# The two-level stage of a transformer block on one core: operands loaded six units ahead, level-1 differences a unit earlier, chunk loads a unit earlier, normalisation tiles overlapped

## The chip, the cores and the metric

The kernel runs on one core of one Trainium2 chip. The metric is the device time of one execution in microseconds (us), the median of several runs. A profiled execution of the same program gives the trace that is read here. The engines are TensorE (PE: matmuls; PEld: its weight loads), VectorE (DVE), ScalarE (ACT), GpSimd (POOL) and SyncE (SP), whose queue issues all DMAs.

## The reference

One block: layer norm with a modulation, an attention with a memory over four segments, a residual; a second layer norm, a gated feed-forward (GEGLU), a residual. Everything is float32. The change lies in the second half.

```python
def _B_ref(x, w_gate, w_up, w_down):        # x 2048 x 1024, F = 3584
    return (_gelu(x @ w_gate) * (x @ w_up)) @ w_down

mod = (_silu(c) @ w_mod).reshape(c.shape[0], 6, 1, -1)
sa, ca, ga, sb, cb, gb = (mod[:, 0], mod[:, 1], mod[:, 2], mod[:, 3], mod[:, 4], mod[:, 5])
h = _layernorm(x, axis=-1) * (1 + ca) + sa
x = x + ga * _A_ref(h, A_wq, A_wk, A_wv, A_wo, A_beta)
h = _layernorm(x, axis=-1) * (1 + cb) + sb
x = x + gb * _B_ref(h, B_w_gate, B_w_up, B_w_down)
```

## The kernel before

**Precision.** Every matmul operand is split into an upper half (a ScalarE copy to fp32r) and a lower half (source minus upper half, on VectorE or GpSimd); three matmuls make one product. `cut` and `put_two` do this; `put_two` issues the lower half only behind the next operand's upper half (`owed`, `settle`).

**Fast multiplication.** gate and up are computed with a scheme of seven products instead of eight (Strassen's in Winograd's form), numbered 1 to 7 and worked in the order `ROUND` = 1, 5, 6, 2, 7, 3, 4. Four of the seven products of the outer level are carried out with a second level inside; that is the stage here, `two(n)` for n = 0 to 27, called a **unit**. Units 0 to 13 work on the operand pair 1 and 2 (the first pair), units 14 to 27 on the pair 5 and 6 (the second). A unit is 14 products of 6 matmuls, 84 in all: for each r in `ROUND` one product for each operand of the pair. It ends in four partial results per operand, which go to DRAM (`st_d`). In a second-pair unit the sums continue from base values loaded back from there (`base_load`, tiles `y`). Behind the stage come 56 **chunks** (`gate_up(u)`), 36 matmuls each, for the outer level's products 7, 3 and 4, and then `down()`.

**What sets the order.** The program is written out by Python generators. `sides` is a list of them; `step()` runs behind every product and advances each by one `yield`. So a `yield` is a step of 6 matmuls, and 14 steps are a unit. `later(k, f)` calls f k steps on. PE's, VectorE's, ScalarE's, GpSimd's and SP's instructions stand in the order in which they are written, and each engine works its queue in that order. An instruction that waits holds all that stand behind it on its engine, and this holds for DMAs on SP.

The parts that the change touches:
- `norm_steps`, with `wait=6`: the second layer norm of the last segment, four token tiles, beside units 1 to 5. One tile is loaded, scaled, transposed on PE in two halves (`turn`, tiles `tpc` in the single PSUM bank `o`) and evacuated to `htc` by ScalarE (first half) or VectorE (second half).
- `mixes`: sums and differences of the normalised rows for both levels, stored to DRAM as `mix_d`: `a_mix(0)`, `a_mix(1)` (when the norm is done), `a_mix_two` (those of the second pair).
- `a_second`: loads the second pair's 14 operands of 512 KB (tiles `w`) and splits each into two, 28 in all (`AA`). An operand takes the place of a first-pair operand when unit 13 has used it (`done`).
- `b_two(n)` makes unit n's weights (`BB`) beside unit n - 1 from raw rows `g` and calls `seven`, whose four sums GpSimd makes. For the second pair GpSimd first takes the level-1 differences of up and gate (with `gh`) and stores one of them (`t2_d`).
- `a_last`: the chunks' operands (`ra`, split to `A`); `gu_load`: a chunk pair's raw weights (`ru`, `rg`); `b_part`: their splits (`B`); `cg_load`: a chunk's three partial results (`cg`).

## Time and profile before

| what | us |
|---|---|
| median of 3 runs (2709.99 to 2714.82) | 2712.97 |
| the profiled execution, its own time | 2714.43 |
| its span | 2712.5 |
| start of unit 1, 13, 14, 15 | 1142.29, 1386.91, 1410.61, 1451.94 |
| start of chunk 0, of `down()` about | 1702.52, 2191.7 |

The page gives the busy time of each engine over the span, the chain of waits (followed back from the last instruction to what released each), and groups of like instructions by line. `out<-in` are tile names without numbers; x12 is a count. In a row of waits stand the total, the number of times and the longest; in a timeline the start, the duration and, in brackets, the idle time before and what ended it; in a table of windows the busy time (count) of each engine, then the granted TensorE clock, the DMA engines' share and GB/s. The time of the whole is set by TensorE where it has matmuls ready; where it waits, the last releaser is what counts.

### The profile page before, as it was taken

To read this page: it belongs to the slowest core of one execution; us is meant where nothing else is said; L and a number is where in the kernel's file an instruction comes from. 1 tells how busy PE (TensorE), PEld (TensorE's weight loads), DVE (VectorE), ACT (ScalarE), POOL (GpSimd) and SP (SyncE) were. 2 spreads that over 40 slices of the span, in tenths; PEclk is the share of its full clock that TensorE was granted. 3 is DMA by queue.
4 is the path that set the end of the run, shared out by engine and by line. 5 is a ranking of instruction groups with operands and counts; after the bars stand their busy time and mean duration, and the time that the engine had idled before them with its cause. 6 is when DMAs were issued, how large, how long until landed. Compare 5 with 4: busy or idle time off the path is not lost.

```text
span 2712.5 us, 42405 instructions
## 1 busy us (share of the span) xinstructions
PE 2644.9 (98%) x13905; PEld 2193.3 (81%) x13905; DVE 1746.8 (64%) x3681; ACT 1377.4 (51%) x3163; POOL 1046.6 (39%) x1586
## 2 busy tenths in 40 slices
PE   7999999999999999999998999899999999999999
PEld 6788888888888788777876888688888888888887
DVE  6676656766677745767775555677777554575456
ACT  6778767776767634555553334433333333233323
POOL 4233334433343532334456665387787300000000
PEclk9999999999999999999998999899999999999999
DMA  7355444435443567577887777899999896786563
GB/s 264 103 157 159 116 135 141 144 102 159 114 133 99 174 213 245 185 258 259 284 313 255 271 273 273 324 358 370 361 360 366 297 342 222 270 296 202 184 209 123
DMA packets 284187, 617.81 MB, mean 228 GB/s; under 512 B 28992, under 2 KB 53568, under 8 KB 283968
## 3 DMA queue, kind: packets, MB, share of 16 engines
q1 hardware_dynamic: 283968, 615.13, 67.4%
q8 instruction: 109, 1.79, 0.3%
q14 instruction: 110, 0.90, 0.1%
HBM read 378.56 MB, written 186.12 MB: 208 GB/s over the span
## 4 chain that ended last, share of the span: by engine, by line
PE 47%; DMA 3%; DVE 2%; issue 1%; ACT 1%; POOL 0%; SPq 0%; ACTq 0%; DVEq 0%; POOLq 0%
PE y L1647 19%; PE f L1446 16%; PE pb L1226 5%; PE pa L1226 3%; PE pc L1226 3%; DMA w<-mix_d 1%; DMA cg<-st_d 0%; DMA wr<-gd_d 0%; DMA rg<-wg 0%; DVE y L1254 0%; ACT BB L934 0%; DMA ra<-mix_d 0%; DMA rm<-h_d 0%; DMA ru<-wu 0%; DMA hid_d<-g 0%
## 5 line engine op out<-in xcount | busy, mean ns | idle before, releaser
L1647 PE MATMUL y<-B,L 128*128 128x512 f32 x2352 | 533.9, 389 | 0.5 <-DVE L L931 0.5
L1647 PEld LDWEIGHTS y<-B,L 128*128 128x128 f32 x2352 | 441.3, 188 | 93.0 <-DVE L L931 1.2
L1446 PE MATMUL f<-A,B 128*128 128x512 f32 x2016 | 462.7, 391 | 9.2 <-DVE A L931 7.0
L1446 PEld LDWEIGHTS f<-A,B 128*128 128x128 f32 x2016 | 380.0, 189 | 91.7 <-DVE A L931 9.8
L619 ACT ACTIVATE sj<-sj,mm 128x384 f32<-128x384 f32 (+3 forms) x512 | 281.0, 552 | 41.0 <-DVE mm L617 40.5
L706 POOL TENSOR_SCALAR_AFFINE_SELECT pt<-pt 128x128 f32<-128x128 f32 x512 | 166.8, 347 | 331.5 <-ACT pt L705 323.5
L617 DVE CUSTOM_DVE_ANT_0 sj<-S,mask 128x384 f32<-128x384 f32 (+3 forms) x512 | 228.2, 488 | 98.5 <-PE S L615 71.5
L1226 PE MATMUL pb<-AA,BB 128*128 128x512 f32 x1008 | 252.6, 397 | 16.6 <-POOL AA L931 4.5
L705 ACT ACTIVATE pt<-T 128x256 f32<-128x256 f32 (+3 forms) x512 | 182.3, 444 | 133.1 <-PE T L703 126.5
L1226 PEld LDWEIGHTS pb<-AA,BB 128*128 128x128 f32 x1008 | 190.1, 190 | 64.4 <-DVE AA L931 5.1
L934 ACT ACTIVATE L<-X 128x512 fp32r<-128x512 f32 x168 | 105.8, 630 | 259.1 <-PE y L1647 170.4
L931 DVE TENSOR_TENSOR L<-X,L 128x512 fp32r<-128x512 f32 x168 | 115.9, 691 | 147.1 <-ACT L L934 147.1
L394 POOL TENSOR_TENSOR w<-r,w 128x256 fp32r<-128x256 f32 x180 | 133.7, 773 | 141.4 <-ACT w L388 139.0
L1473 ACT ACTIVATE g<-f 128x512 f32<-128x512 f32 x56 | 33.5, 598 | 287.6 <-PE f L1446 287.6
L403 PE MATMUL kv<-w,hha 128*128 128x256 f32 x896 | 173.8, 284 | 2.2 <-DVE vx L421 2.2
L1226 PE MATMUL pc<-AA,BB 128*128 128x512 f32 x672 | 164.8, 393 | 2.3 <-DVE AA L931 2.2
L1226 PE MATMUL pa<-AA,BB 128*128 128x512 f32 x672 | 164.0, 392 | 0.9 <-DVE AA L931 0.9
L931 DVE TENSOR_TENSOR BB<-g,BB 128x512 fp32r<-128x512 f32 x112 | 91.2, 815 | 95.8 <-ACT BB L934 95.5
L1226 PEld LDWEIGHTS pc<-AA,BB 128*128 128x128 f32 x672 | 126.5, 189 | 30.2 <-DVE AA L931 3.3
L1226 PEld LDWEIGHTS pa<-AA,BB 128*128 128x128 f32 x672 | 126.7, 189 | 28.6 <-DVE AA L931 1.7
L931 POOL TENSOR_TENSOR t_a<-g,t_a 128x256 f32<-128x256 f32 x112 | 91.0, 832 | 150.9 <-DVE BB L931 129.2
L403 PEld LDWEIGHTS kv<-w,hha 128*128 128x128 f32 x896 | 143.9, 191 | 3.4 <-DVE vx L421 2.5
(295 smaller groups left out, 5442.6 us busy)
## 6 DMA issues: line engine op xcount, KB each, us to landing
B<-wc_d SPq DMA_DIRECT2D x112, 512.0 KB, 4.1
cg<-st_d SPq DMA_DIRECT2D x168, 256.0 KB, 6.4
st_d<-x SPq DMA_DIRECT2D x112, 256.0 KB, 2.7
st_d<-y SPq DMA_DIRECT2D x112, 256.0 KB, 2.3
hid_d<-g SPq DMA_DIRECT2D x56, 512.0 KB, 5.9
wc_d<-T SPq DMA_DIRECT2D x56, 512.0 KB, 5.0
X<-hid_d SPq DMA_DIRECT2D x112, 256.0 KB, 4.6
wr<-gd_d SPq DMA_DIRECT2D x84, 256.0 KB, 4.2
```

Of the source, the lines that this page charges most:

```text
L394: nc.gpsimd.tensor_sub(w[:, 1, c], r[:, c], f32(w[:, 0, c]))
L403: nc.tensor.matmul(ps, b[:, sl], w[:, a], start=(kt == 0 and a == 0 and b is hi), stop=(kt == KT - 1 and a == 1), **kw)
L617: nc.vector.tensor_tensor_reduce(out=sj[:, :nv], in0=ps[:, :nv], in1=mask[:, L - nv:], scale=-1.0, scalar=3.4e38, op0=ALU.add, op1=ALU.min ...
L619: nc.scalar.activation(sj[:, :nv], sj[:, :nv], AF.Exp, bias=mm[:, j, i:i + 1], scale=-1.0, accum_out=ll[:, i, j:j + 1])
L705: nc.scalar.activation(pt, ps[:, nn - n:nn], AF.Exp)
L706: nc.gpsimd.affine_select(pt[:, :P], pt[:, :P], pattern=[[1, P]], compare_op=ALU.is_ge, fill=0.0, base=0, channel_multiplier=-1)
L931: f(*xs)
L934: nc.scalar.activation(hi, src, AF.Copy)
L1226: nc.tensor.matmul(ps, w[:, a, at:at + P], A["a", i, r, k][b], start=(r in (1, 5) and k == a == b == 0), stop=(k == 1 and a == 1), skip_gr ...
L1446: nc.tensor.matmul(ps, B[fc, i][:, a, kt * P:(kt + 1) * P], A[p, i, kt][b], start=False, stop=(kt == 3 and a == 1), skip_group_check=True)
L1473: nc.scalar.activation(h2_, pb, AF.Gelu_apprx_tanh)
L1647: nc.tensor.matmul(banks[t], ops[k][:, y, t * P:(t + 1) * P], B[slots[k]][:, x], start=(i not in (2, 4, 3) and j == 0 and x == 0 and y == ...
```

## The change

- **Normalisation:** the next tile's load moves behind this tile's scaling, the halves' transposes stand four steps apart instead of two, and a tile takes 12 steps instead of 17.
- **Second-pair operands:** `a_second` starts five steps behind the end of `mixes` instead of at unit 13, keeps six operands loaded instead of four (two of each six in pairs of `c` tiles), and makes all lower halves on VectorE.
- **Level-1 differences:** a generator of their own, `b_one`, run beside unit n for unit n + 2; in `seven` the third sum of the second pair goes to a temporary instead of over a raw row.
- **GELU and its store** of the first pair's gate: one step later.
- **Ends:** the first four `ra` loads are issued ahead of unit 26, the second chunk pair's raw weights ahead of unit 27, and the middle partial result of the first two chunks with the other two, in a temporary; weights of a unit are finished (`flush`) at its end in all units.

The numbers of lines in the diff and in the rows below are those of each version.

```diff
@@ norm_steps
         if wait:
             for q in range(len(toks)):
-                while stored.get(toks[q]) != 2:
-                    yield
-                load(q)
-                for _ in range(wait):
-                    yield
+                if q == 0:
+                    load(q)
+                    for _ in range(wait):
+                        yield
...
                 norm_scale([t], mv, rs, nm)
-                for _ in range(wait - 2):
+                if q + 1 < len(toks):
+                    load(q + 1)
+                for _ in range(4):
                     yield
-                for h in range(2):
-                    turn(q, h)
+                turn(q, 0)
+                for _ in range(4):
                     yield
-                    yield
+                turn(q, 1)
+                yield
             return
@@ mixes
             yield from a_mix_two()
+            mixed.append(1)
+
+        mixed = []
+
+        def second():
+
+            while not mixed:
+                yield
+            for _ in range(5):
+                yield
+            ff["first"] = a_second()
+            yield from ff["first"]
@@ a_second
-                    t = (ra_tile if q % 4 > 1 else lambda n: pair_tile(n, "U"))(f"w{i}_{r}")
...
+                    if q % 6 > 3:
+                        rs.append([c_tile(f"w{i}_{r}_{c}") for c in range(2)])
+                        for c in range(2):
+                            nc.sync.dma_start(rs[-1][c], src[c * P:(c + 1) * P])
+                        return
+                    t = ra_tile(f"w{i}_{r}") if q % 6 > 1 else flat(pair_tile(f"w{i}_{r}", "U"))
...
-            for _ in range(4):
+            for _ in range(6):
                 load()
...
-                    put_two(i, r, c, rs[q][:, c], nc.gpsimd if c and i == 5 and r in (2, 7, 3, 4) else nc.vector)
+                    put_two(i, r, c, rs[q][c], nc.vector)
@@ b_two, b_one, seven
-            if n >= NJ:
-                for q in (1, 0):
-                    u, g, k = raw[q], raw[2 + q], (2 * (n % NJ) + q) * P
-                    diff(u[:, :L], u[:, :L], g)
-                    yield
-                    diff(u[:, L:], u[:, L:], u[:, :L])
-                    later(1, lambda u=u, k=k: nc.sync.dma_start(t2_d[k:k + P], u[:, L:]))
-                    yield
-                if n + 1 < 2 * NJ:
-                    later(2, lambda: b_two_load(n + 1))
...
-            yield from seven(b11, b12, b21, b22, t1, t2_, put)
+            yield from seven(b11, b12, b21, b22, t1, t2_, put, t1 if n >= NJ else b12)
+
+        def b_one(n):
+
+            b_two_load(n)
+            for _ in range(5):
+                yield
+            for q in range(2):
+                u, g, k = two_raws[n][q], two_raws[n][2 + q], (2 * (n % NJ) + q) * P
+                diff(u[:, :L], u[:, :L], g)
+                yield
+                diff(u[:, L:], u[:, L:], u[:, :L])
+                later(1, lambda u=u, k=k: nc.sync.dma_start(t2_d[k:k + P], u[:, L:]))
+                yield
...
-            diff(b12, b22, b12)
+            diff(t3, b22, b12)
@@ two
-                later(2, lambda: nc.scalar.activation(t, t, AF.Gelu_apprx_tanh))
-                later(3, put)
+                later(3, lambda: nc.scalar.activation(t, t, AF.Gelu_apprx_tanh))
+                later(4, put)
...
-                    cg_load(int(r == 3), (0, 2))
+                    cg_load(int(r == 3), (0, 2, 1))
@@ cg_load
-                t = c_tile(f"cg{q}_{u}") if at < 2 and q != 1 else a_tile(
+                t = tmp_tile(f"cg{q}_{u}") if u < 2 and q == 1 else c_tile(f"cg{q}_{u}") if at < 2 and q != 1 else a_tile(
@@ the loops over units and chunks
                 sides.append([mixes(), 1, "m"])
+                sides.append([second(), 1])
+            if NJ - 2 <= n < 2 * NJ - 2:
+                sides.append([chain(wait_for(3 if n >= NJ else 0), b_one(n + 2)), 1, "o"])
...
             if n == NJ - 1:
                 flush("m")
-                ff["first"] = a_second()
-                sides.append([ff["first"], 1])
...
+            if n == 2 * NJ - 2:
+                following.append(a_last())
+                next(following[0])
             if n == 2 * NJ - 1:
-                following.append(a_last())
                 sides.append([following[0], 1])
-            if 0 < n < NJ - 1:
+            if 0 < n < NJ - 2:
                 b_two_load(n + 2)
-            elif n == 2 * NJ - 2:
-                gu_load(0)
+            elif n >= 2 * NJ - 2:
+                gu_load(n - 2 * NJ + 2)
             two(n)
-            if n < NJ - 1:
-                flush("b")
+            flush("b")
+            flush("o")
         for u in range(NU):
             fc, p = divmod(u, 2)
             if p == 0 and fc + 1 < FC:
+                sides.append([b_part(fc + 1), 1, "b"])
                 if fc + 2 < FC:
                     gu_load(fc + 2)
-                sides.append([b_part(fc + 1), 1, "b"])
-            if u == 0:
-                cg_load(0, (1,))
-                cg_load(1, (1,))
```

**SP's queue around the second pair's first loads** (`w`, the name's first number is r; `st_d` stores of unit 12's results, `t_d` the stored level-1 differences). Before:

```order
L1000 DMA mix_d_76<-u_1_0_17047 128x512
L1263 DMA st_d_73<-y_1_17108 128x512
L1263 DMA st_d_74<-x_0_17142 128x512
L1121 DMA w_1_17236<-mix_d_70 128x2x512
L1121 DMA w_1_17238<-mix_d_70 128x2x512
L1121 DMA w_5_17240<-mix_d_75 128x2x512
L1121 DMA w_5_17242<-mix_d_76 128x2x512
L1263 DMA st_d_74<-y_0_17154 128x512
L1162 DMA t_d<-g_1_17052 128x512
L1121 DMA w_6_17290<-mix_d_75 128x2x512
```

and now:

```order
L1014 DMA mix_d_76<-u_1_0_16953 128x512
L1285 DMA st_d_73<-x_0_17150 128x512
L1196 DMA t_d<-g_0_17070 128x512
L1140 DMA w_1_17167<-mix_d_70 128x2x512
L1140 DMA w_1_17169<-mix_d_70 128x2x512
L1140 DMA w_5_17171<-mix_d_75 128x2x512
L1140 DMA w_5_17173<-mix_d_76 128x2x512
L1136 DMA w_6_0_17175<-mix_d_75 128x512
L1136 DMA w_6_1_17176<-mix_d_75 128x512
L1285 DMA st_d_74<-x_1_17105 128x512
L1196 DMA t_d<-g_1_17071 128x512
```

The loads stand ahead of seven of unit 12's eight result stores instead of behind seven, six operands deep (two more of unit 13's operand 6 follow the last `w` row shown), but behind the store of a level-1 difference, `t_d<-g_0`.

**GpSimd's queue in unit 14** (`g` level-1 differences, `t_a` sums in `seven`, `AA` lower halves of operands; x2 is the two halves of a row). Before:

```order
L931 TENSOR_TENSOR g_1_17338<-g_1_17338,gh_1_17343 128x256 x2
L931 TENSOR_TENSOR AA_2_1_1_17477<-w_2_17367,AA_2_1_0_17476 128x256 x2
L931 TENSOR_TENSOR g_1_17338<-g_1_17338 128x256 x2
L931 TENSOR_TENSOR g_0_17337<-g_0_17337,gh_0_17340 128x256 x2
L931 TENSOR_TENSOR g_0_17337<-g_0_17337 128x256 x2
L931 TENSOR_TENSOR t_a_17551<-g_1_17338,g_0_17337 128x256 x2
L931 TENSOR_TENSOR AA_7_1_1_17548<-w_7_17431,AA_7_1_0_17547 128x256 x2
L931 TENSOR_TENSOR t_a_17552<-g_1_17338,t_a_17551 128x256 x2
L931 TENSOR_TENSOR g_1_17338<-g_1_17338 128x256 x2
L931 TENSOR_TENSOR AA_3_1_1_17625<-w_3_17497,AA_3_1_0_17624 128x256 x2
L931 TENSOR_TENSOR t_a_17552<-g_0_17337,t_a_17552 128x256 x2
L931 TENSOR_TENSOR AA_4_1_1_17674<-w_4_17573,AA_4_1_0_17673 128x256 x2
```

and now:

```order
L933 TENSOR_TENSOR t_a_17510<-g_1_17263,g_0_17262 128x256 x2
L933 TENSOR_TENSOR t_a_17511<-g_1_17263,t_a_17510 128x256 x2
L933 TENSOR_TENSOR t_a_17510<-g_1_17263 128x256 x2
L933 TENSOR_TENSOR t_a_17511<-g_0_17262,t_a_17511 128x256 x2
L933 TENSOR_TENSOR g_0_17567<-g_0_17567,gh_0_17570 128x256 x2
L933 TENSOR_TENSOR g_0_17567<-g_0_17567 128x256 x2
L933 TENSOR_TENSOR g_1_17568<-g_1_17568,gh_1_17573 128x256 x2
L933 TENSOR_TENSOR g_1_17568<-g_1_17568 128x256 x2
```

The four `AA` rows are gone to VectorE; the differences that unit 14's GpSimd makes are no longer those that its own sums `t_a` need but those of the unit behind.

**SP's queue between unit 27 and chunk 1** (`ru`, `rg` raw weights; `cg` partial results; `ra` operands). Before, from the middle of the first group of raw weights:

```order
L1347 DMA rg_19960<-wg 128x512
L1348 DMA rg_19960<-t_d 128x512
L1340 DMA cg_1_19964<-st_d_73 128x512
L1340 DMA cg_1_19966<-st_d_74 128x512
L1340 DMA cg_0_19968<-st_d_73 128x512
L1340 DMA cg_1_19970<-st_d_73 128x512
L1340 DMA cg_2_19972<-st_d_73 128x512
L1263 DMA st_d_74<-y_0_19786 128x512
L1346 DMA ru_19988<-wu 128x1024
L1347 DMA rg_19989<-wg 128x512
L1348 DMA rg_19989<-t_d 128x512
L1316 DMA ra_4_0_20004<-h_d 128x2x512
```

and now:

```order
L1338 DMA ra_3_1_19966<-mix_d_71 128x2x512
L1368 DMA ru_19972<-wu 128x1024
L1369 DMA rg_19973<-wg 128x512
L1370 DMA rg_19973<-t_d 128x512
L1362 DMA cg_0_19977<-st_d_73 128x512
L1362 DMA cg_1_19979<-st_d_73 128x512
L1362 DMA cg_2_19981<-st_d_73 128x512
L1285 DMA st_d_74<-y_0_19798 128x512
L1338 DMA ra_4_0_20010<-h_d 128x2x512
L1338 DMA ra_4_1_20039<-h_d 128x2x512
```

One group of raw weights and two `cg` loads have left this place; they stand in unit 27.

8 lines of the change are left out of this document (4 added, 4 removed).

## The prediction

> **What bounds the kernel now.** I read the page first, for the engine that is always busy.
>
> ```profile
> span 2712.5 us, 42405 instructions
> PE 2644.9 (98%) x13905; PEld 2193.3 (81%) x13905; DVE 1746.8 (64%) x3681; ACT 1377.4 (51%) x3163; POOL 1046.6 (39%) x1586
> ```
>
> TensorE (PE) is busy for 98%, so only time that PE loses can be won. The change touches the stage of 28 units (line 1226) and the first two chunks behind it. I cut that stretch with the table of windows at the starts of units 1, 13, 14 and 15, of the chunk stage, and of its first undisturbed run of matmuls.
>
> ```profile
> core 0: us, PE busy (x) PEld busy (x) DVE busy (x) ACT busy (x) POOL busy (x), PEclk, DMA share, GB/s
> 1142.29:1386.91 244.62, 235.61 (x1042) 191.27 (x1040) 169.29 (x252) 134.36 (x249) 113.30 (x127) 1.00 0.80 275
> 1386.91:1410.61 23.70, 20.09 (x86) 15.45 (x84) 14.42 (x21) 12.76 (x25) 10.27 (x12) 1.00 0.90 306
> 1410.61:1451.94 41.33, 28.17 (x85) 18.38 (x84) 30.23 (x37) 20.23 (x38) 33.40 (x37) 0.78 0.79 276
> 1451.94:1702.52 250.58, 250.58 (x1097) 206.35 (x1096) 143.80 (x205) 99.25 (x180) 148.66 (x184) 1.00 0.77 271
> 1702.52:1732.94 30.42, 21.27 (x72) 14.63 (x70) 18.01 (x26) 12.80 (x24) 7.37 (x8) 0.78 0.89 337
> ```
>
> The chain of waits gives the price of a group of 12 matmuls:
>
> ```profile
> 1282.74 2.72 PE pb L1226 x12
> 1285.46 2.72 PE pc L1226 x12
> ```
>
> A unit is 84 matmuls, so 7 x 2.72 = 19.04 us; one step (6 matmuls) is 1.36 us. Against that:
> - **Start**, units 1 to 12: 244.62 - 12 x 19.04 = 16.1 us too long. Eight groups of transposes at about 0.41 us (1162.85 to 1163.26 below) are 3.3 of it; 12.8 us are lost.
> - **Pair change**, units 13 and 14: 23.70 + 41.33 = 65.03 us instead of 38.08; 26.95 us lost. The granted clock of 0.78 in unit 14 is inside this sum.
> - Units 15 to 27: no loss (PE busy all 250.58 us).
> - **End**: 70 matmuls (70 x 0.2267 = 15.87 us) take 30.42 us; 14.55 us lost.
>
> Together 54.3 us are to be had. PE's waits name the releasers:
>
> ```profile
> PE tpc L269 <- ACT htc L278: 7.1, 4, 2.6
> PE f L1446 <- DVE A L931: 7.0, 4, 3.9
> PE pb L1226 <- POOL AA L931: 4.5, 1, 4.5
> PE pb L1226 <- DVE AA L931: 3.4, 3, 1.7
> PE pb L1226 <- ACT x L1250: 2.5, 1, 2.5
> PE f L1446 <- ACT A L934: 2.1, 1, 2.1
> ```
>
> **Part 1, the normalisation (start).** PE's timeline shows one token tile:
>
> ```profile
> 1162.85 0.66 PE L269 MATMUL tpc<-ident,nc 128*128 128x128 f32 x4 [0.47 <-ACT nc L248]
> 1163.26 3.01 PE L1226 MATMUL pa<-AA,BB 128*128 128x512 f32 x12
> 1168.51 0.66 PE L269 MATMUL tpc<-ident,nc 128*128 128x128 f32 x4 [2.24 <-ACT htc L278]
> ```
>
> The second half's transposes need the single "o" bank, which ScalarE empties of the first half 1168.51 - 1163.26 = 5.25 us after its transposes. Before, 12 matmuls (2.72 us) stand between the halves, and PE waits for the rest. Now 24 stand there (5.44 us), so the waits of 7.1 us go but for about 0.2 us. ScalarE's GELU also moves one step back, so that it is less often blocked there. The tile takes 12 steps instead of 17; its work is the same and lies under matmuls. **Term: -7** (bounds -3, if the denser work makes the evacuations later, to -9, if some of the unnamed 5 us go too). The mixed operands are stored 11 steps sooner (60 steps of the first mix instead of 71 of the normalisation stand before the second mix); the next part needs that.
>
> **Part 2, the pair change.** Here is what the 28 second-pair operands (AA, 14 loads of 512 KB) cost now; ScalarE's and POOL's timelines, the queue's, and four pieces of the chain:
>
> ```profile
> 1391.46 2.01 SPq L1121 DMA_DIRECT2D w<-mix_d  x4
> 1397.25 0.63 ACT L1015 ACTIVATE AA<-w 128x512 fp32r<-128x512 f32 x1 [3.85 <-DMA w<-mix_d]
> 1419.54 1.87 POOL L931 TENSOR_TENSOR AA<-w,AA 128x256 fp32r<-128x256 f32 x2 [5.44 <-ACT AA L1015]
> ...
> 1391.46 5.76 DMA w<-mix_d
> 1406.53 7.75 DMA w<-mix_d
> 1423.28 4.05 DMA t_d<-g
> 1434.81 7.94 DMA w<-mix_d
> ```
>
> The loads are issued 4.5 us into unit 13, four deep, and ScalarE, which is in order, stands behind them; later loads wait for one of four buffers, land 7.75 and 7.94 us after issue, and four lower halves queue on POOL behind level-1 differences that wait for DMAs. The change answers each: the first loads are emitted at about step 8 of unit 12 instead of the first step of unit 13, six steps (8 us) sooner, so that the first should land near 1397.25 - 8 = 1389.2, 2.3 us into unit 13; a load is issued five operands (10 steps, 13.6 us) before its use instead of three (8.2 us), against landings of at most 7.94 us; the lower halves all go to VectorE; the differences come a unit earlier, in a temporary that the store does not hold. The extra four DMAs cost an issue each (w x4 above: 2.01 / 4 = 0.5 us) on SP, which has room.
>
> What is late next is **VectorE**. In the new order 56 VectorE instructions stand from the first lower half to the last. They may run from about 2.5 us into unit 13 (first landing) until one step before the end of unit 14: 38.08 - 2.5 - 1.4 = 34.2 us. Their mean is not known beforehand; the nearest rows are 14.42 / 21 = 0.687 us (POOL busy 43%) and 30.23 / 37 = 0.817 us (POOL busy 81%). That is 38.5 to 45.8 us, 4.3 to 11.6 too many; POOL's 16 instructions a unit will lie between, so I take the middle, 8, and 1 us for one hand-over from ScalarE to VectorE (0.63 and 0.69 us) at the last operands. Of the 26.95 us, 9 stay. **Term: -18** (bounds -23, with 4.3 us left, to -13, with 14 left should loads be late too). The DMA engines set a similar floor:
>
> ```profile
> DMA packets 9428, 18.66 MB, mean 287 GB/s; under 512 B 848, under 2 KB 848, under 8 KB 9424
> 1800.00:1850.00 50.00, 50.00 (x222) 41.42 (x221) 33.04 (x40) 18.63 (x36) 37.09 (x40) 1.00 0.99 372
> ```
>
> Units 13 and 14 moved 18.66 MB. Less six early loads (3.1 MB), 15.5 MB at 372 GB/s (the rate of a full window) take 41.7 us: 3.6 over, below VectorE's 47.
>
> **Part 3, the end.**
>
> ```profile
> 1709.39 4.21 SPq L1340 DMA_DIRECT2D cg<-st_d  x5
> 1717.29 1.00 SPq L1316 DMA_DIRECT2D ra<-h_d  x2
> 1716.63 0.69 DVE L1470 TENSOR_TENSOR g<-cg,cg 128x512 f32<-128x512 f32 x1 [5.42 <-DMA cg<-st_d]
> 1717.98 3.78 PE L1446 MATMUL f<-A,B 128*128 128x512 f32 x8 [3.93 <-DVE A L931]
> 1715.25 5.81 DMA ru<-wu
> 1722.66 0.63 ACT L934 ACTIVATE B<-ru 128x512 fp32r<-128x512 f32 x1 [8.79 <-POOL ru L931]
> 1726.86 4.22 PE L1446 MATMUL f<-A,B 128*128 128x512 f32 x9 [2.21 <-DVE A L931]
> ```
>
> Two late loads hold everything: part 1 of the first chunk (VectorE waits 5.42 us with A's lower halves behind it) and the raw weights of the next chunk (ScalarE waits 8.79 us with A's upper halves behind it). Both are now issued in unit 27, before 1702.52 and so at least 7 us sooner; both in-order queues run on. Late next is the last operand, ra_4 of the second half: it was issued at 1717.29; five fewer DMAs stand ahead of it, at 4.21 / 5 = 0.84 us each 4.2 us, so I expect 1713.1 and, with 4.1 us (the base load's landing in the steady units, quoted under C) to land and 1.3 us to split, 1718.5, when its product could start at 1702.52 + 5 x 2.72 = 1716.1. About 2.5 us stay. **Term: -12** (bounds -8, with two waits of 3 us left, to -14). The four ra loads move into unit 26; 2.1 MB more on 271 GB/s x 19 us = 5.1 MB stays under 372 x 19 = 7.1 MB.
>
> **Edits at nothing.** In units 15 to 26 POOL keeps 16 instructions a unit (148.66 us of 250.58) and now waits for VectorE before it overwrites a temporary; VectorE idles 43% there and PE waits for neither. If that cover failed, rival C is its price. The early flush only empties generators that are done by then.
>
> Sum: 7 + 18 + 12 = 37 us off the profiled execution's 2714.43 us; that is 1.5 us above the median of the runs (2712.97), so **2676 us**. The terms' bounds give 24 to 46 us, 2667 to 2689.
>
> **Rivals.** A, *VectorE against POOL*. The nearest row for an instruction with both operands in SBUF while POOL works is 1205 ns:
>
> ```profile
> L1254 DVE TENSOR_TENSOR y<-y,x 128x512 f32<-128x512 f32 x3 | 3.6, 1205 | 0.1
> L931 DVE TENSOR_TENSOR AA<-w,AA 128x512 fp32r<-128x512 f32 x24 | 21.0, 883 | 6.0 <-ACT AA L1015 6.0
> ```
>
> If all 43 such instructions of the 56 (28 AA, 13 BB, 2 sums) took that, 43 x 1.205 + 13 x 0.683 = 60.7 us, 26.5 over: part 2 gives nothing, 2694 us. Against it: AA's mean was 883 ns with POOL at 81%. 8%. The Trainium skill's page "SBUF — State Buffer", section "SBUF: two separate sides", says that VectorE with two SBUF inputs and GpSimd share a port as an exclusive lock, the loser waiting for the whole instruction; by that rule the halves moved off POOL would pay up to A's price. The trace agrees that the wait exists (1205 against about 683 ns) and not that each pays it.
>
> B, *the loads do not come sooner*. In the new order they stand behind a store of a level-1 difference, which waits for POOL. If that holds SP as long as the before's start of 1391.46, only POOL's own 4.5 us and some of the rest go, part 2 gives 8 us: 2686 us. For it: SP is in order. Against: POOL was busy only 10.27 of 23.70 us in unit 13, and that difference is its sixth of about eight in unit 12. 10%.
>
> C, *slower*: the difference's store, at step 10 of a unit, holds SP in units 15 to 26 until the base sums' load (step 2 of the next unit, used five steps = 6.8 us later) is late. That needs a hold of over six steps, 8.2 us; then each of 12 units would wait for one landing of a base load,
>
> ```profile
> y<-st_d SPq DMA_DIRECT2D x44, 256.0 KB, 4.1
> SPq L1162 <- POOL t_a L931: 2.1, 7, 0.3
> ```
>
> 12 x 4.1 = 49 us, more than the 37 gained: 2725 us. Against: from 1460 to 1680 those stores held SP 2.1 us in all. 4%.
>
> **How the numbers follow.** Forecast 76%, A 8%, B 10%, C 4%, 2% for what I do not see. The range 2666 to 2695 takes in the bounds, A and B. What a measurement can tell from no change is about 0.2% (5.4 us). Faster 0.94 (forecast, A, B), same 0.02, slower 0.04 (C).
>
> **What would show it.** Part 1 is right if PE's wait for htc falls from 7.1 to under 1 us. Part 2: units 13 and 14 take about 47 us together, ScalarE no longer waits for w near the start of unit 13, POOL no longer appears as PE's releaser, and VectorE is busy almost throughout. Part 3: the wait of 5.42 us for cg and of 8.79 us for ru are gone, and the 70 matmuls take 18 to 19 us. Units 15 to 27 must still be 250 us. It is wrong if the two units still take over 55 us (A or B: VectorE's mean against the time of the first w load tells which), or if the steady units show waits for y.

## The result and the profile after

| | before | after |
|---|---|---|
| median, us | 2713.89 (2709.99 to 2716.85) | 2688.66 (2683.83 to 2691.29) |
| the profiled execution, its span | 2714.43, 2712.5 | 2689.39, 2687.5 |
| ratio of the times | | 0.9906, 95% interval 0.9887 to 0.9925 |

The changed kernel is 0.94% faster, about 25 us. The page of the changed kernel still has TensorE busy almost throughout:

```profile
span 2687.5 us, 42440 instructions
PE 2635.1 (98%) x13905; PEld 2188.8 (81%) x13905; DVE 1742.5 (65%) x3685; ACT 1382.0 (51%) x3163; POOL 1043.0 (39%) x1578
```

The table of windows of the changed kernel, cut at the same events as before: starts of units 1, 13, 14, 15, of the chunk stage, and of its 71st matmul.

```profile
1139.85:1382.20 242.35, 235.19 (x1041) 191.44 (x1040) 173.72 (x256) 137.92 (x252) 120.79 (x132) 1.00 0.84 285
1382.20:1403.46 21.26, 19.63 (x85) 15.61 (x84) 14.57 (x20) 14.31 (x28) 12.89 (x15) 1.00 1.04 381
1403.46:1435.61 32.15, 23.89 (x85) 15.02 (x84) 29.04 (x40) 18.17 (x35) 19.91 (x20) 0.98 0.84 291
1435.61:1686.01 250.40, 250.40 (x1098) 206.50 (x1096) 141.45 (x205) 102.31 (x180) 153.19 (x189) 1.00 0.78 275
1686.01:1708.04 22.03, 18.14 (x72) 13.90 (x70) 16.23 (x24) 11.80 (x21) 4.05 (x4) 0.92 1.05 405
```

| stage | before | after | gain | forecast |
|---|---|---|---|---|
| up to unit 1 (unit 0 included) | 1142.29 | 1139.85 | 2.4 | 0 |
| units 1 to 12 | 244.62 | 242.35 | 2.3 | 7 |
| units 13 and 14 | 65.03 | 53.41 | 11.6 | 18 |
| units 15 to 27 | 250.58 | 250.40 | 0.2 | 0 |
| 70 matmuls of the chunk stage | 30.42 | 22.03 | 8.4 | 12 |
| the rest | 979.56 | 979.46 | 0.1 | 0 |

The gains add up to the 25.0 us between the spans. Not all of them are waits that went. In units 13 and 14 TensorE's busy time for the same 168 matmuls fell from 20.09 + 28.17 = 48.26 to 19.63 + 23.89 = 43.52 us, 4.7 of the 11.6 us; in the 70 matmuls of the end from 21.27 to 18.14, 3.1 of the 8.4. The granted clock rose in the same rows (0.78 to 0.98 in unit 14, 0.78 to 0.92 at the end); how much of the shorter busy time is the clock's the rows do not separate.

TensorE's waits in the changed kernel, from 1100 to 1800 us:

```profile
PE pb L1248 <- DVE AA L933: 4.9, 8, 2.3
PE pb L1248 <- DVE x L1274: 4.7, 5, 1.9
PE pb L1248 <- DVE y L1274: 4.3, 4, 2.8
PE f L1468 <- ACT A L936: 3.4, 1, 3.4
```

The waits for `htc` (7.1 us before) and for POOL's lower half (4.5) have gone, and that for VectorE's `A` (7.0) but for 0.5 us. Three others stand there: VectorE's operand halves (AA), VectorE's evictions of partial sums (x, y), and one last chunk operand at ScalarE.

**Start.** Within the start of unit 1 to that of unit 13, VectorE's waits in the changed kernel and SP's:

```profile
DVE m L973 <- DMA rm<-h_d: 28.7, 7, 6.3
SPq L964 <- DMA mix_d<-rm: 10.8, 4, 3.9
```

Before, VectorE waited 11.9 us for these rows (`rm`, the mixes' inputs). Their load waits on SP until the last store from the same buffer has landed. The evictions stand behind these waits on VectorE, and TensorE behind the evictions: by the order of the queues that is the y and x of TensorE's waits.

**Pair change.** SP's first load, and VectorE's work from the first lower half to the last:

```profile
1375.76 2.00 SPq L1140 DMA_DIRECT2D w<-mix_d  x4
```

```profile
1386.04 0.69 DVE L933 TENSOR_TENSOR AA<-w,AA 128x512 fp32r<-128x512 f32 x1
...
1397.54 0.69 DVE L1280 TENSOR_TENSOR y<-pa,x 128x512 f32<-128x512 f32 x1 [3.25 <-DMA st_d<-y]
...
1427.62 3.28 DVE L933 TENSOR_TENSOR AA<-w,AA 128x512 fp32r<-128x512 f32 x3
...
1433.33 1.20 DVE L933 TENSOR_TENSOR AA<-w,AA 128x512 fp32r<-128x512 f32 x1
```

The first load goes out 6.4 us ahead of unit 13 (1382.20), where before it went out 4.5 us behind its start. From 1386.04 to the end of the last half at 1434.53 are 48.5 us; the prediction had room for 34.2. One wait of 3.25 us, for a `y` tile that is still being stored, stands in unit 13; from there on VectorE has next to no gap until 1431.

**End.** The last operand of the second half (two loads), on SP, on ScalarE and on TensorE (the three rows are from the timelines of the three engines):

```profile
1696.48 1.69 SPq L1338 DMA_DIRECT2D ra<-h_d  x2
1703.03 1.15 ACT L936 ACTIVATE A<-ra 128x512 fp32r<-128x512 f32 x2 [1.34 <-DMA ra<-h_d]
1703.71 0.50 PE L1468 MATMUL f<-A,B 128*128 128x512 f32 x1 [3.38 <-ACT A L936]
```

It is issued 10.5 us into the stage, as forecast, but ScalarE can take it only 6.5 us later, where 4.1 had been put in. The waits of 5.42 us for `cg` on VectorE and of 8.79 us for `ru` on ScalarE are gone.

### The profile page after: what moved, and what is told of

It reads as the page before. It is cut to its first block, busy times and chain, and to the rows that moved or that the text cites. A ratio compares the mean times of both kernels' runs of the same rounds, so it can differ in the third digit from the quotient of the medians.

```text
span 2687.5 us, 42440 instructions
## 1 busy us (share of the span) xinstructions
PE 2635.1 (98%) x13905; PEld 2188.8 (81%) x13905; DVE 1742.5 (65%) x3685; ACT 1382.0 (51%) x3163; POOL 1043.0 (39%) x1578
## 4 chain that ended last, share of the span: by engine, by line
PE 88%; DMA 5%; DVE 4%; ACT 2%; issue 2%; POOL 0%; SPq 0%; DVEq 0%; ACTq 0%; POOLq 0%
PE y L1669 19%; PE f L1468 16%; PE kv L405 9%; PE pb L1248 6%; PE q L411 6%; PE y L783 6%; PE pa L1248 4%; PE pc L1248 4%; PE S L617 3%; PE T L705 3%; PE O L717 3%; PE kT L524 2%; PE vT L524 2%; DMA rm<-h_d 1%; PE num L673 1%
## 5 line engine op out<-in xcount | busy, mean ns | idle before, releaser
L1248 PE MATMUL pb<-AA,BB 128*128 128x512 f32 x1008 | 250.8, 395 | 15.2 <-DVE AA L933 4.9
L933 DVE TENSOR_TENSOR BB<-t_a,BB 128x512 fp32r<-128x512 f32 x98 | 78.6, 802 | 86.3 <-ACT BB L936 86.2
```

What stands on the lines that cost most here:

```text
L933: f(*xs)
L1248: nc.tensor.matmul(ps, w[:, a, at:at + P], A["a", i, r, k][b], start=(r in (1, 5) and k == a == b == 0), stop=(k == 1 and a == 1), skip_gr ...
```

## The experiments

Twelve kernels, each an edit of the changed kernel except *gelu_only*, which is an edit of the kernel before. Times are medians; ratios are to the kernel before. The stages are read from each run's own profile:

| kernel | median | ratio, 95% interval | units 1 to 12 | 13 and 14 |
|---|---|---|---|---|
| gelu_back | 2698.23 | 0.9952 (0.9937 to 0.9967) | 251.70 | 56.77 |
| norm_back | 2694.39 | 0.9940 (0.9925 to 0.9955) | 236.03 | 67.53 |
| lows_pool | 2688.52 | 0.9911 (0.9892 to 0.9931) | 241.92 | 56.42 |
| lead4 | 2683.68 | 0.9902 (0.9886 to 0.9918) | 240.06 | 52.96 |
| seq_soon | 2698.17 | 0.9950 (0.9935 to 0.9964) | 252.89 | 51.26 |
| gelu_only | 2697.48 | 0.9945 (0.9931 to 0.9959) | 236.25 | 60.18 |
| diffs_late | 2686.34 | 0.9908 (0.9892 to 0.9924) | 239.99 | 53.60 |
| mix_store | 2690.39 | 0.9921 (0.9904 to 0.9938) | 243.59 | 54.52 |
| mixes_soon | 2686.08 | 0.9906 (0.9889 to 0.9922) | 236.15 | 57.31 |
| bb_pool | 2685.46 | 0.9903 (0.9888 to 0.9917) | 240.45 | 52.88 |
| gu_late | 2691.92 | 0.9927 (0.9912 to 0.9942) | 240.94 | 52.97 |
| mixes_order | 2680.86 | 0.9878 (0.9861 to 0.9896) | 236.16 | 52.04 |

How far one profile can be trusted: lows_pool, lead4, diffs_late, bb_pool and gu_late have the changed kernel's code in units 1 to 12, and with it they span 239.99 to 242.35 us. (lead4 differs in two loads in unit 12, which takes 19.04 us in both.) A difference under 2.4 us in that stage is no finding. The changed kernel's own 242.35 is the longest of the six, so its 2.3 us against the kernel before (one profile, 244.62) could by the others be up to 4.6. Units 13 and 14 repeat within 1.6 us where their code is the same (53.41, gu_late 52.97, mix_store 54.52).

**gelu_back.**

```diff
-                later(3, lambda: nc.scalar.activation(t, t, AF.Gelu_apprx_tanh))
-                later(4, put)
+                later(2, lambda: nc.scalar.activation(t, t, AF.Gelu_apprx_tanh))
+                later(3, put)
```

> The changed kernel with GELU two steps and its store three steps after the sum, as before (the change has three and four). Theory: in the changed kernel VectorE waits 3.25 us at 1397.54 in unit 13 for a y tile that is still being stored, because that store now goes out a step (1.36 us) later into full DMA queues; with the old distances the wait falls to under 2 us and units 13 and 14, 53.41 us in the changed kernel, lose 1.5 to 3 us (50.5 to 52). Rival: the store is late because the DMA engines are full (busy share 1.04 in unit 13), not because it is issued a step later; then the wait stays within 0.7 us and so do the two units. A second rival: GELU a step sooner blocks ScalarE ahead of VectorE's second sum; then the stage of units 1 to 12 (242.35 us) or 15 to 27 (250.40 us) grows by over 1 us.

The wait for the stored `y` tile went (VectorE's longest but for weights' halves is now 3.2 us, for a product of TensorE's), but the two units grew by 3.4 us instead of shrinking: the theory missed. The second rival, thought of as a side effect, was the large one: units 1 to 12 took 9.4 us more. So the GELU edit, which the prediction gave no price, is worth more than its whole first term. TensorE does not wait for `htc` here either: the distance between a tile's halves does remove that wait, as forecast. But TensorE's waits in these units are for other things now (8.1 us for VectorE's `y` and `x`, 3.5 for the scaled tile), and the stage is longer than before (251.70 against 244.62).

**gelu_only** puts that edit alone (GELU, and its store with it) into the kernel before.

```diff
-                later(2, lambda: nc.scalar.activation(t, t, AF.Gelu_apprx_tanh))
-                later(3, put)
+                later(3, lambda: nc.scalar.activation(t, t, AF.Gelu_apprx_tanh))
+                later(4, put)
```

> The kernel before with one edit alone: GELU three steps after the sum (for two) and its store four steps after it (for three). The prediction costed this edit at nothing. Theory: ScalarE, in order, stands at GELU until VectorE's second sum is done (waits of 51.9 and 31.5 us in units 1 to 12 of the kernel before), and VectorE meanwhile waits for ScalarE's upper halves (54.4 us); a step later the sum is done in time. Units 1 to 12 fall from 244.62 to 235.5 to 238 us, all other stages stay within 1.5 us, and the kernel gains 6 to 9 us. Rival: the effect seen with GELU put back (251.7 against 242.35 us) exists only together with the overlapped normalisation; then units 1 to 12 stay within 1.5 us of 244.62.

The theory held: 8.4 us in units 1 to 12 and, beyond what was expected, 4.9 us in units 13 and 14. By the medians taken side by side, 2711.17 - 2697.48 = 13.7 us come from this edit alone, over half of the change's gain. ScalarE's waits in the kernel before, units 1 to 12:

```profile
ACT y L1267 <- DVE y L1254: 51.9, 24, 3.9
ACT y L1267 <- issue: 31.5, 12, 5.1
```

and in gelu_only ScalarE's longest, then TensorE's:

```profile
ACT y L1267 <- DVE y L1254: 22.3, 20, 2.4
```

```profile
PE tpc L269 <- ACT htc L278: 2.3, 2, 1.2
```

L1267 is GELU. It waits for the second of VectorE's two sums, and whatever stands behind it on ScalarE, the weights' upper halves and the evacuation of `htc`, waits too. A step later the sum is mostly done. TensorE's waits for `htc` fall from 7.1 to 2.3 us without any change to the normalisation: two thirds of the wait on which the prediction built its term for the overlap were GELU's. What the expectation said of VectorE was not borne out: its wait for ScalarE's upper halves went only from 54.4 to 52.6 us.

**norm_back** restores the old `norm_steps`.

```diff
-                if q == 0:
-                    load(q)
-                    for _ in range(wait):
-                        yield
+                while stored.get(toks[q]) != 2:
+                    yield
+                load(q)
+                for _ in range(wait):
+                    yield
...
-                if q + 1 < len(toks):
-                    load(q + 1)
-                for _ in range(4):
-                    yield
-                turn(q, 0)
-                for _ in range(4):
-                    yield
-                turn(q, 1)
-                yield
+                for _ in range(wait - 2):
+                    yield
+                for h in range(2):
+                    turn(q, h)
+                    yield
+                    yield
```

> The changed kernel with the four normalisation tiles one after the other, as before. Theory: the overlap took away TensorE's waits for htc (7.1 us), but the mixes' row loads came next, and VectorE's waits for them rose from 11.9 to 28.7 us, so that units 1 to 12 gained 2.3 us of 7. Then with the old order TensorE's htc waits come back at 6 to 8 us, VectorE's waits for the rows fall below 20 us, and units 1 to 12 take 244 to 245.5 us against 242.35. The prediction's own size would be 249 us. Rival: the gain of 2.3 us in that stage came from something else (the second pair's loads, or the raw weights moved out of it); then the stage stays within 0.7 us of 242.35 although the htc waits are back. Units 13 and 14 may grow if the mixes end later; under 2 us expected.

Neither size was right. The stage became *shorter*, 236.03 us: the overlap costs it 6.3 us instead of gaining 2.3 or 7. VectorE's wait for the mixes' rows did fall, from 28.7 to 13.7 us, and TensorE's waits for VectorE's `y` and `x` (3.7 and 1.9 us in the changed kernel) are gone; for `htc` only 2.3 us came back. In all TensorE waits 4.1 us less in this stage and is busy 2.2 us less (235.19 to 233.00), which makes up the 6.3. The two edits make a square. Units 1 to 12 in the windows of gelu_back, gelu_only and norm_back:

```profile
1134.63:1386.33 251.70, 238.71 (x1042) 191.96 (x1041) 172.24 (x255) 134.07 (x249) 118.69 (x132) 0.99 0.79 271
1140.82:1377.07 236.25, 233.10 (x1041) 192.02 (x1040) 169.02 (x254) 141.58 (x251) 117.51 (x130) 1.00 0.83 285
1138.93:1374.96 236.03, 233.00 (x1042) 192.09 (x1040) 170.09 (x255) 140.71 (x251) 117.57 (x130) 1.00 0.82 284
```

| units 1 to 12 | tiles in sequence | tiles overlapped |
|---|---|---|
| GELU two steps on | 244.62 (before) | 251.70 (gelu_back) |
| GELU three steps on | 236.25 (gelu_only), 236.03 (norm_back) | 242.35 (after) |

GELU's step gains 8.4 to 9.4 us in either column; the overlap costs 6.1 to 7.1 in either row (with the other five profiles of the changed kernel's code in the last cell, 3.7 to 5.9 in the lower row). Units 13 and 14, however, took 14 us more without the overlap. Units 13 and 14 in norm_back's table of windows, and the `w` loads in its view of that tile (count, duration in ns, first and last start in us):

```profile
1374.96:1442.49 67.53, 50.21 (x169) 34.15 (x168) 46.94 (x60) 33.28 (x62) 35.31 (x37) 0.84 0.80 288
```

```profile
L1138 SPq DMA_DIRECT2D w<-mix_d x10: 370/414/1056, 1383.0 to 1419.8; - x10
```

The first `w` load goes out 8 us behind the start of unit 13, because the mixes end later and `a_second` stands behind them. This is the overlap's worth: not a wait less, but an earlier end of the mixes.

**seq_soon** tries to have both: norm_back's edit with the tiles drawn together (`wait=5`), and the loads three steps behind the mixes.

```diff
-                sides.append([norm_tiles(x1_d, h2_d, (3,), 4, 3, "c", wait=6, get=ra_tile), 1, "m"])
+                sides.append([norm_tiles(x1_d, h2_d, (3,), 4, 3, "c", wait=5, get=ra_tile), 1, "m"])
-            for _ in range(5):
+            for _ in range(3):
                 yield
             ff["first"] = a_second()
```

> The changed kernel with the normalisation tiles one after the other as before, but with one step less ahead of each (5 for 6) and one less behind its scaling, and with the second pair's loads three steps (not five) after the end of the mixes: the first load then stands about 6 steps ahead of unit 13, as in the changed kernel, and not behind its start as with the old order alone. Theory, formed from the runs with GELU and with the normalisation put back: the overlap costs units 1 to 12 some 6 us (242.35 us with it, 236.03 without) and its worth is only that the mixes end sooner, so that the second pair's first load comes sooner (units 13 and 14: 53.41 us with it, 67.53 without). Then here units 1 to 12 take 235 to 238 us, units 13 and 14 52 to 55 us, and the kernel is 4 to 8 us faster than the changed one. Rival: units 1 to 12 are as long as the mixes are dense, whichever way the tiles stand; then they take 241 to 243 us and nothing is gained. A second rival: the two units depend on the overlap itself (the tiles' buffers), not on the first load; then they take over 60 us.

Units 13 and 14 came out as the theory said and even shorter (51.26 us, unit 13 without any loss), so the first load's place is what counts there, not the overlap. Units 1 to 12 came out at 252.89, worse than either order. TensorE's first wait in units 1 to 5 of seq_soon says why:

```profile
PE tpc L269 <- ACT nc L248: 7.4, 4, 3.6
```

With three steps between a tile's scaling and its transposes TensorE waits for the scaled tile (0.7 us in norm_back, which has four), and the rest of those units is crowded too (VectorE waits 15.2 us for `rm`, 7.2 in norm_back). Dense work hurts there, not the order of the tiles.

**mix_store** stores each mix's fourth result after one step, to shorten the chain of store, load and sum.

```diff
-                    later(3, lambda i=i, t=t, kt=kt: nc.sync.dma_start(mix_rows(p, i)[kt * P:(kt + 1) * P], t))
+                    later(1 if i == 3 else 3, lambda i=i, t=t, kt=kt: nc.sync.dma_start(mix_rows(p, i)[kt * P:(kt + 1) * P], t))
```

> The changed kernel with the store of each mix's fourth result one step after its sum instead of three. Theory: the next row's load waits on SP for this store's landing (10.8 us in 4 waits in units 1 to 12), and VectorE then waits for the load (28.7 us in 7 waits) with the evictions behind it; two steps (2.7 us) less in that chain take VectorE's waits for the rows below 15 us, and units 1 to 12 (242.35 us) lose 2 to 5 us. Rival: the store waits for VectorE on SP instead and holds the stores and loads behind it, so the row loads come no sooner; then the stage stays within 1 us, and SP's wait for VectorE at the mixes' stores (31.9 us) grows.

The theory missed. SP's wait for the landing of `mix_d<-rm` fell from 10.8 to 4.1 us, and VectorE's for the rows stayed (28.9 us): the store's place is not what holds the rows. The stage did not gain (243.59, 1.2 us more, within the spread of these profiles). That is the rival's outcome, but hardly by its way: SP's wait for VectorE at the mixes' stores went from 31.9 to 32.5 us only. The rows took 5.3 us in the median from issue to landing (6.0 in the changed kernel); that this transfer itself is what they wait for is likely and was not tested.

**lead4** keeps four operands loaded ahead instead of six.

```diff
-                    if q % 6 > 3:
...
-                    t = ra_tile(f"w{i}_{r}") if q % 6 > 1 else flat(pair_tile(f"w{i}_{r}", "U"))
+                    t = ra_tile(f"w{i}_{r}") if q % 4 > 1 else flat(pair_tile(f"w{i}_{r}", "U"))
...
-            for _ in range(6):
+            for _ in range(4):
                 load()
```

> The changed kernel with four of the second pair's operands loaded ahead instead of six (the other 24 loads as they come free). Theory: the first loads' earlier place is what helped, and six ahead cover landings of up to 8 us under load; with four ahead ScalarE waits for w again and units 13 and 14 (53.41 us) grow by 3 to 6 us. Rival: VectorE is behind by more than a landing through unit 14 anyway, so that two loads less ahead cost under 1 us; and since 1 MB less is pushed into unit 13's full DMA queues (busy share 1.04), the 3.25 us wait for the stored y tile even falls, and the two units stay within 1 us or gain up to 2.

ScalarE's first wait in units 13 and 14 of lead4:

```profile
ACT AA L1029 <- DMA w<-mix_d: 10.4, 5, 4.0
```

ScalarE does wait for `w` again, and it costs nothing: the two units take 52.96 us. The two operands more bring nothing that these runs can show.

**lows_pool** gives the four lower halves back to POOL:

```diff
-                    put_two(i, r, c, rs[q][c], nc.vector)
+                    put_two(i, r, c, rs[q][c], nc.gpsimd if c and i == 5 and r in (2, 7, 3, 4) else nc.vector)
```

> The changed kernel with the four lower halves of operands that stood on POOL before back on POOL (the other 24 stay on VectorE). Theory: VectorE is the bound from 1397.5 to 1431, where it never idles; four instructions of 0.85 to 1.2 us less there let units 13 and 14 (53.41 us) fall by 2 to 4 us. Rival, the reason for which the prediction took them off POOL: they queue on POOL behind level-1 differences that wait for DMAs, and TensorE waits for POOL again; then the two units take 54 us or more, and POOL appears as TensorE's releaser with over 2 us.

The rival, and with it the prediction's reason for that edit. TensorE's first wait in units 13 and 14 of lows_pool:

```profile
PE pb L1248 <- POOL AA L933: 5.9, 2, 3.1
```

The two units took 3 us more. The kernel's median (2688.52) does not show 3 us against the changed one; that is within the spread of the runs. So the 3 us rest on one profile of each kernel, in a stage that repeats within 1.6 us.

**bb_pool** spares VectorE other work, that no DMA holds:

```diff
             def put(r, src, eng):
+                eng = nc.gpsimd if n in (NJ, NJ + 1) and r in (5, 7, 3) else eng
                 t = b_tile(f"BB{n}_{r}")
```

> The changed kernel with three of the seven lower halves of the weights' splits (products 5, 7 and 3) of units 14 and 15 on POOL instead of VectorE. Theory: VectorE is the bound of the pair change, without a gap from 1397.5 to 1431; six instructions of 0.69 to 1.23 us less on it, and none of them behind a DMA, let units 13 and 14 (53.41 us) lose 2 to 5 us. Rival: an instruction on POOL lengthens those on VectorE beside it as much as it spares (its halves took 0.68 us alone and up to 1.29 beside POOL); then the two units stay within 1 us. A second rival: POOL's work queues and TensorE waits for POOL's halves, as it did for the operands' halves put back there (56.42 us); then they take over 55 us.

The two units of bb_pool and those of the changed kernel in one window each:

```profile
1379.50:1432.38 52.88, 43.94 (x170) 30.48 (x169) 43.46 (x53) 32.57 (x62) 41.90 (x43) 0.99 0.87 318
```

```profile
1382.20:1435.61 53.41, 43.52 (x169) 30.63 (x168) 43.60 (x59) 32.48 (x62) 32.80 (x34) 0.99 0.92 327
```

VectorE has 53 instructions instead of 59 and is busy as long: 43.46 / 53 = 0.820 us each against 43.60 / 59 = 0.739. What six instructions less would have spared is given back by the longer ones that stay, while POOL is busy 9 us more. The first rival.

**diffs_late** delays unit 16's differences inside unit 14.

```diff
-                sides.append([chain(wait_for(3 if n >= NJ else 0), b_one(n + 2)), 1, "o"])
+                sides.append([chain(wait_for(6 if n == NJ else 3 if n > NJ else 0), b_one(n + 2)), 1, "o"])
```

> The changed kernel with unit 16's level-1 differences three steps (4.1 us) later inside unit 14 (six steps after its start for three). Theory: VectorE's last lower halves in unit 14 take 1.1 to 1.2 us each from 1427.6 on, against 0.68 just before, because POOL works on these differences from 1423.2 to 1432 without a break; later differences let them run at 0.68 to 0.75 us, and units 13 and 14 (53.41 us) lose 1 to 2.5 us. Rival: POOL has its own products to make in the same stretch, which then lie there in place of the differences: the two units stay within 0.7 us. The differences could also come too late for unit 16; then unit 15 (20.15 us) grows by over 1 us.

No change (53.60 us): in diffs_late the last three lower halves, VectorE's row

```profile
1423.64 3.27 DVE L933 TENSOR_TENSOR AA<-w,AA 128x512 fp32r<-128x512 f32 x3
```

still take 1.09 us each. But the theory was not put to the test. POOL's rows in diffs_late:

```profile
1421.93 2.15 POOL L933 TENSOR_TENSOR g<-g,gh 128x256 f32<-128x256 f32 x2 [6.29 <-DMA gh<-wg]
1424.04 2.32 POOL L933 TENSOR_TENSOR g<-g 128x256 f32<-128x256 f32 x2
1426.32 1.88 POOL L933 TENSOR_TENSOR g<-g,gh 128x256 f32<-128x256 f32 x2
```

The differences start 22.5 us into unit 14 (from 1399.46), for 19.8 in the changed kernel, and wait for `gh` in both; the three halves stand 24.2 us into it in both, so POOL still works on these differences beside them. Whether the halves are shorter without them, or POOL's sums would take their place as the rival says, stays open.

**gu_late** loads the chunks' raw weights where they were before.

```diff
-            elif n >= 2 * NJ - 2:
-                gu_load(n - 2 * NJ + 2)
+            elif n == 2 * NJ - 2:
+                gu_load(0)
...
-                sides.append([b_part(fc + 1), 1, "b"])
                 if fc + 2 < FC:
                     gu_load(fc + 2)
+                sides.append([b_part(fc + 1), 1, "b"])
```

> The changed kernel with the chunks' raw weights loaded where they were before, within the chunk stage, and the rest of the end as changed (part 1 of the first chunks with the other parts, operands' loads a unit sooner). Theory, the prediction's: two late loads held the end, one after the other, 5.42 us at VectorE and 8.79 us at ScalarE; with the raw weights late again ScalarE waits for them 6 to 9 us with the operands' upper halves behind it, and the 70 matmuls of the end, 20.46 us in the changed kernel, take 25 to 30. Rival: with the part-1 loads out of SP's way the raw weights come some 4 us sooner also from their old place, and the last operand, which lands 6.5 us after its issue, is what bounds the stage; then it takes 20 to 23 us.

ScalarE's first wait at the end of gu_late, and the window there:

```profile
ACT B L936 <- POOL ru L933: 7.9, 1, 7.9
```

```profile
1683.40:1711.27 27.87, 18.74 (x72) 13.47 (x70) 17.21 (x24) 11.49 (x21) 7.37 (x8) 0.88 0.88 336
```

The theory: 27.87 us against 22.03 (the expectation's 20.46 is to the 67th matmul, not to the 71st). Of the 8.4 us that the end gained, 5.8 hang on the raw weights' place; 30.42 - 27.87 = 2.6 remain for the other end edits together.

**mixes_soon** takes the normalisation in its old order and finds the early end elsewhere, in the later mixes:

```diff
# a_mix
-                    for _ in range(5 if i == 3 and p == 0 else 2):
+                    for _ in range((5 if i == 3 else 2) if p == 0 else 1 if i in (7, 3) else 2):
# a_mix_two
-                        for _ in range(2):
+                        for _ in range(1 if r in (7, 3) else 2):
```

> The changed kernel with the normalisation tiles in the old order and spacing, and the mixes behind them drawn together instead: in the passes after the first one step less behind the third and behind the last of each four sums, 16 steps in all, so that the second pair's first load stands at about the start of unit 12. Theory: the overlap costs some 6 us in units 1 to 12 (242.35 us with it, 236.03 without), dense work in units 1 to 5 being what hurts (closer tiles: 252.89), and it pays only by an early first load; units 6 to 12 have room for denser mixes. Then units 1 to 12 take 235.5 to 238 us, units 13 and 14 51 to 55 us, and the kernel is 3 to 7 us faster than the changed one (2682 to 2686 us by its median of 2688.66). Rival: density hurts wherever it stands; then units 6 to 12, all at 19.04 us without the overlap, grow by over 3 us together and nothing is gained.

Units 1 to 12 as the theory said (236.15; from unit 6 on each takes 19.04), so density there costs nothing. But units 13 and 14 took 57.31 us for the 51 to 55 expected, 26.02 of them in unit 13. From mixes_soon's waits between 1360 and 1433 us, VectorE, POOL and SP:

```profile
DVE y L1278 <- DMA st_d<-y: 4.4, 1, 4.4
POOL g L931 <- DMA gh<-wg: 16.9, 3, 11.0
SPq L1194 <- POOL g L931: 15.8, 6, 5.9
```

The eight early `w` loads now stood on SP ahead of the raw weights of unit 15; the differences waited for those, the differences' stores held SP, the stores of the sums stood behind, and VectorE waited for a `y` tile not yet stored. That is the prediction's rivals B and C in small: SP held by a store that waits for POOL.

**mixes_order** moves the eight loads behind the raw weights, one number:

```diff
-            for _ in range(5):
+            for _ in range(11):
                 yield
             ff["first"] = a_second()
```

> The kernel of mixes_soon with one number changed: the second pair's loads stand eleven steps (for five) behind the end of the mixes, so that on SP they come behind the raw weights' loads of unit 15 and not ahead of them. Theory: in mixes_soon the eight early loads (2.8 + 2.5 us of issue, 3 MB) held the raw weights back, POOL waited 16.9 us for gh, the differences' stores held SP (15.8 us) with the sums' stores behind them, and VectorE stood 4.4 us at a y tile that was still being stored; unit 13 took 26.02 us. With the loads behind, unit 13 takes 19 to 21.5 us, units 13 and 14 together 51 to 54 us (57.31 before this edit), units 1 to 12 stay at 236 to 237 us, and the kernel comes out at 2678 to 2683 us by the measure in which the changed kernel has 2688.66 (6 to 10 us faster than it). Rival: what holds unit 13 is the early end of the mixes or the DMA queues' load as such, not the place of the eight loads; then unit 13 stays over 24 us, and the time at 2685 to 2688.

The windows of units 1 to 12, 13 and 14 in mixes_order:

```profile
1139.49:1375.65 236.16, 233.02 (x1042) 192.05 (x1040) 175.50 (x256) 140.83 (x252) 120.86 (x132) 1.00 0.87 299
1375.65:1394.69 19.04, 19.04 (x85) 15.72 (x84) 16.13 (x20) 14.30 (x28) 13.71 (x14) 1.00 0.96 332
1394.69:1427.69 33.00, 23.59 (x86) 14.75 (x84) 30.86 (x40) 18.18 (x35) 21.93 (x22) 1.00 0.83 289
```

Unit 13 has no loss left, and the kernel, 2680.86 us (2675.49 to 2681.79), is faster than both: 1.2% below the kernel before, and some 8 us below the changed one, whose fastest run was 2683.83. The two were not timed side by side; their intervals to the kernel before overlap (0.9861 to 0.9896, 0.9887 to 0.9925), the ranges of their runs do not.

## Why the prediction was right, and where it was not

The direction held and the time lay in the range; the gain was 25 us where 37 were forecast, each of the three terms too large. That the time lay in the range is in part luck: the terms' bounds ended at 2689 us and the kernel has 2688.66, nearer to rival B's 2686, which did not come (the first load went out 6.4 us ahead of unit 13), than to the forecast's 2676. And 10 us (gelu_back against the changed kernel) to 14 us (gelu_only) of the 25 are the GELU edit's, which no term priced: without it the change has 2698.23 us, above the range's end of 2695.

- **Part 1 (-7, measured -2.3): the step that failed.** It read 7.1 us of waits for `htc` and gave them to the distance between a tile's halves. gelu_only shows that 4.8 of them were ScalarE standing at GELU, an edit the prediction mentions in half a sentence and does not price. Its sign, a wait for `htc` under 1 us, came true, and the time did not follow, because the wait moved to VectorE's evictions (gelu_back, norm_back). In fact the overlap costs some 4 to 7 us and GELU's step gains 8 to 12, by which profiles one takes; that the sum of the two lies near the term's lower bound of 3 is luck. That the mixes end sooner and the next part needs it was right, and is all that the overlap gives.
- **Part 2 (-18, measured -11.6, outside the bounds of -13 to -23).** That the loads had to come sooner was right (norm_back: 14 us hang on it), and so was POOL (lows_pool: 3 us). That VectorE is late next was right, too: TensorE waits for its halves, and it is busy 29.04 of 32.15 us in unit 14. The sizes were not: the window of 34.2 us took 48.5. VectorE's mean was inside the assumed range (0.739 us). And part of the 11.6 is GELU's: that edit alone gains 4.9 us here (gelu_only), so that the other edits add 60.18 - 53.41 = 6.8 on top of it, or 65.03 - 56.77 = 8.3 without it (gelu_back). What was left out is that VectorE itself waits: 3.25 us for a `y` tile behind the late stores, some 5 us for weights' upper halves, and its start came at 3.8 us into unit 13 instead of 2.5. Loading five operands ahead of use was given as a cause, and lead4 shows none of it.
- **What stays of unit 14.** It took 31.3 to 34.5 us in all these kernels (the changed one, lows_pool, mixes_order and the others with early loads) instead of 19.04. Weights' halves moved from VectorE to POOL (bb_pool) and differences started 2.7 us later (diffs_late) did not help. `a_second` writes out one operand half a step, 28 in 28 steps, so that the last ones come just when they are due; a faster pace there was not tried, and whether it would help is open.
- **Part 3 (-12, measured -8.4).** Mechanism and issue time (10.5 us into the stage for 10.6) were right, and the two waits went. The sign of 18 to 19 us for the 70 matmuls was missed (22.03). The last landing was mis-sized, 6.5 us where 4.1 stood, with the DMA engines at a share of 1.05; and the last ten of the matmuls, from 1703.71 to 1708.04, took 4.3 us where the sum has 10 x 0.2267 = 2.3. gu_late shows that the raw weights carry 5.8 of the 8.4.
- **Edits at nothing.** Units 15 to 27 took 250.40 us (250.58 before): right. Rival C did not come. Rival A is there in the small: VectorE's instructions beside POOL are longer, not all of them at 1.2 us. The 883 ns set against it are the mean over units 13 and 14, in which POOL was busy 67% (43.67 of 65.03 us); in unit 14 alone, with POOL at 81%, the row has

```profile
L931 DVE TENSOR_TENSOR AA<-w,AA 128x512 fp32r<-128x512 f32 x17 | 15.7, 933 | 0.0
```

- Ahead of unit 1 2.4 us were gained, to which the prediction gave no term. In the twelve runs unit 1 starts at 1134.63 to 1140.82; what moves it was not followed.

## What to carry to other kernels

A wait of TensorE for an engine that works in order names the last releaser, not the culprit: look at what stood ahead of the released instruction on that engine, and price that edit by itself, even when it moves one instruction by one step. Overlapping work that already had room makes a crowded stretch more crowded; if its worth is that something ends early, take the earliness from a stretch that has slack, as mixes_order does. And the place of loads in the one issuing queue counts against the loads behind them as much as for their own users.

## What the runs showed of the hardware that was not expected

- Six 128x512 subtractions moved from VectorE to GpSimd left VectorE's busy time as it was (43.60 us for 59 instructions, 43.46 for 53). It is no fixed exchange: in lows_pool four subtractions less on VectorE did bring its busy time down, to 41.18 us for 55. What gets longer is the form with both inputs in SBUF; the evictions of `pa`, `pb` and `pc`, which read one input from PSUM, stay at 675 to 692 ns in the changed kernel, bb_pool and lows_pool. Two rows of bb_pool's units 13 and 14:

```profile
L933 DVE TENSOR_TENSOR AA<-w,AA 128x512 fp32r<-128x512 f32 x28 | 26.3, 963 | 1.4 <-ACT AA L1029 1.1 <-DMA t_d<-g 0.3
L1271 DVE TENSOR_TENSOR y<-pc,y 128x512 f32<-128x512 f32 x2 | 1.4, 686 | 0.8 <-PE pc L1249 0.8
```
- The rule of the Trainium skill that rival A cites ("SBUF — State Buffer", section "SBUF: two separate sides"), a lock between GpSimd and a VectorE instruction with two SBUF inputs, held for the whole instruction by the one that starts first, points the same way. The trace does not show every such instruction paying for it. VectorE's timeline in the changed kernel, and POOL's:

```profile
1425.52 0.67 DVE L933 TENSOR_TENSOR AA<-w,AA 128x512 fp32r<-128x512 f32 x1
...
1427.62 3.28 DVE L933 TENSOR_TENSOR AA<-w,AA 128x512 fp32r<-128x512 f32 x3
```

```profile
1423.24 2.34 POOL L933 TENSOR_TENSOR g<-g,gh 128x256 f32<-128x256 f32 x2 [3.60 <-DMA gh<-wg]
1425.55 2.52 POOL L933 TENSOR_TENSOR g<-g 128x256 f32<-128x256 f32 x2
1428.04 2.31 POOL L933 TENSOR_TENSOR g<-g,gh 128x256 f32<-128x256 f32 x2
```

POOL works without a break beside both, and the same form takes 0.67 us once and 1.09 us each of three times.
- With the DMA engines at a share of 1.05 and 405 GB/s, a 512 KB operand load at the end took 6.5 us from issue to use, where a base load of 256 KB in the steady units of the kernel before (share 0.77, 271 GB/s) took 4.1 in the median. The two differ in size and in load; which of them counts is not shown.
